# One GpSimd cast per head pair becomes a transfer, and the written-out order of all instructions is searched anew

## The chip, the cores and the metric

The kernel runs on one core of one Trainium2 chip. The metric is device microseconds of one execution. Three runs of the kernel before took 751.69, 751.89 and 752.91 us, with a median of 751.89 us.

The core's engines are TensorE (PE, with PEld for its weight loads), VectorE (DVE), ScalarE (ACT) and GpSimd (POOL). Each works through its own list of instructions in the order in which it stands; they meet only at semaphores. SyncE (SP) issues all transfers here. A row of SP is the issue of a transfer, and the transfer itself runs on the DMA engines.

## The reference

Two layers for 8 batches, 8 heads, 576 tokens, 64 columns per head. The first is causal attention with a bias from running sums of `s`; the second is a channel mix with 512 and 1024 columns:

```
scores = q @ k.T / 8                       # per head, 576 x 576
cum    = cumsum(max(s, 0))
scores = where(causal, -1e9, scores + min(cum_k - cum_q, 0))
x      = softmax(scores) @ v               # heads side by side: (8, 576, 512)
xk = mu_k * x + (1 - mu_k) * x_previous_token     # xr the same with mu_r
k  = relu(xk @ w_k)
out = sigmoid(xr @ w_r) * (k * k @ w_v)
```

Products are made exact by splitting: an operand is a rounded high part and a low part (what the rounding left), and two or three products of parts are added in PSUM.

## The kernel before, in words

**Attention.** The heads go in pairs. The first batch is done in two visits per pair (tiles A: queries 0 to 319; Z: the rest) and the second batch in one; these are the "plain" visits, whose weights TensorE turns (L1695) before it sums the values (`sum_plain`, L1816). From the third batch on (`b >= BY_DMA`, BY_DMA is 2) `split_scores` makes the scores (L1390), VectorE takes the row minimum (L1402), ScalarE the exponentials (L1417), ScalarE and VectorE write high and low halves of the weights (L1442, L1448), a transposing transfer turns them (L1535), and `sum_values` sums the values of both heads of the pair in one block of 32 matmuls (L1576).

**Keys and queries.** `split_qk` prepares a head: GpSimd (or ScalarE in the first two batches) rounds the keys into half of the tile `KH` (L1224, L1227, L1231), GpSimd writes the rest into the other half (L1235), and a second copy of the rounded keys goes into `KL` (L1241), beside three rows of running sums that a transfer brings (L1216). The queries are treated likewise (`G` at L1251 or L1255, `QL` at L1259). One product takes `KH` and `G`, the second `KL` and `QL`. The pair's heads are j = 0 and j = 1; `KH` and `KL` have three buffers each.

**Channel mix.** Tokens go in 18 chunks of 256. For the first two batches x goes through memory and is mixed and split by ScalarE and VectorE (L1993 to L2037); for the later ones `mix_pair` does it from the value sums (L1621 to L1669). `hidden` makes xk @ w_k (L2065, 96 matmuls of 256 columns per chunk), then relu (L2079), square and split; `gate` makes xr @ w_r (L2142); `output` makes the product with w_v (L2196), multiplies by the gate (L2207) and stores. The weights are first taken from 64-bit words, scaled by a power of two and split into halves (L940 to L1030).

**The order.** No engine's order is written by hand. The body of the kernel only records tasks in `Plan`: engine, planned length in ns, what it reads and writes, a due time. `pe`, `act`, `dve`, `pool` and `dma` turn columns into a planned length. `Plan.run` then makes the order: due times with a random shift drawn from SEED, PASSES rounds of `forward` (a list scheduler: at each step the engine that is free first takes the ready task with the earliest due time) and `backward` (new due times from the end), and then a nudge of the due times in one stretch for each number of CHAIN. The last `forward` gives each engine's order, and, for tasks with a choice (`or_act`, `or_dve`, `or_pool`), the engine. Where the planner sees TensorE idle ahead of the first two-part score product (L1315), it places a small matmul on the identity (`one_idle`, L540), whose result nobody reads.

The SP queue is in order too: each transfer's issue waits there for its sources and for the landing of a transfer eight before it.

Of the kernel before, what the change touches and what calls it, by code (L numbers as in the profile page):

```python
# [30 lines left out]
def f32(ap):  # L31
    return ap.bitcast(F32)
# [22 lines left out]
class Plan:  # L55
# [239 lines left out]
    def backward(self, start, on):  # L295
# [43 lines left out]
        return [-x for x in at]  # L339


    PASSES, SEED = 45, 67
    SHIFTS = 500.0, 2000.0, 5000.0, 10000.0
    NUDGES, SPANS = (300.0, 1000.0, 3000.0, 8000.0), (5000.0, 15000.0, 40000.0)
    LENGTH = 740000.0
    CHAIN = (
# [26 lines left out]
    )  # L373
    engines = ('DVE', 'ACT', 'POOL', 'SP', 'PE')
    LATER = 300.0
# [33 lines left out]
def forgetting_attention_then_channel_mix(  # L409
# [16 lines left out]
    nc = tc.nc  # L426

    B, H, D, S = q.shape
# [20 lines left out]
    def sbuf(shape, tag, bufs=1, dtype=F32):  # L449
        return plan.buffer(sb, shape, dtype, tag, bufs)  # L450
# [17 lines left out]
    def at_quarters(i, quarters):  # L468
        if quarters != (0, 0):
            plan.quarters[i] = quarters  # L470
        return i
# [12 lines left out]
    def pool(emit, reads, writes, n, extra, rate=0.8333, quarters=(0, 0)):  # L484
        return at_quarters(plan.add("POOL", n * rate + extra, emit, reads, writes), quarters)
# [12 lines left out]
    def dma(emit, reads, writes, ns):  # L498
        return plan.add("SP", 1.286 * ns, emit, reads, writes, land=1300)
# [75 lines left out]
    BY_DMA = 2  # L575
# [529 lines left out]
    ALL, A, Z = tuple(range(NQ)), (0, 1, 2), (3, 4)  # L1105
# [95 lines left out]
    def split_qk(b, hp, qs, k):  # L1201
# [4 lines left out]
        nq, nk = qs[0].n, k.n  # L1206
        found = []
        for j in range(2):
            own, other = slice(64 * j, 64 * j + 64), slice(64 - 64 * j, P - 64 * j)
            QQ, K = (sbuf([P, n], x, 3, F32R) for n, x in ((nq, "G"), (nk, "KH")))  # L1210
            QL, KB = (sbuf([P, S], x, 3, F32R) for x in ("QL", "KL"))
# [17 lines left out]
            else:  # L1229
# [7 lines left out]
                ),  # L1237
                [(k, j), (K, j)], [(K, 1 - j)], nk, 210, 1.99, (2 * j, 2 - 2 * j),
            )
            pool(  # L1240
                lambda own=own, KB=KB: nc.gpsimd.tensor_copy(KB.get()[0:64, 0:nk], k.get()[own]),  # L1241
                [(k, j)], [(KB, 0)], nk, 150, 0.8333, (2 * j, 0),
            )
            x = qs[j]
            if b < BY_DMA:
                or_pool(
# [300 lines left out]
    def sum_values(Ts, V):  # L1547
# [25 lines left out]
        def all_of_it():  # L1573
# [21 lines left out]
        columns = sum(n - start(y, kb) for y, x, kb in todo) + 4 * 64  # L1595
        pe(
            all_of_it, [(V, 0), (V, 1)] + list(dict.fromkeys(keys)), [found], columns, 64,
            1.05 / 2.4 + 256 / columns,
        )
        return found  # L1600

# [185 lines left out]
    def sum_plain(phs, rinv, V, xT, tiles):  # L1787
# [25 lines left out]
        def all_of_it():  # L1813
# [33 lines left out]
        columns = (q1 - q0) / 2 + sum(q1 - max(q0, kb * P) for kb in range(blocks))  # L1847
        pe(
            all_of_it, [V, ident16, (r16, 0), (r16, 1)] + keys, some, columns, 64,
            4 / 2.4 - 10 / columns,  # L1850
        )
        for a, e, sums, invs, off in places:
            def x(a=a, e=e):
# [653 lines left out]
```

## Time and profile before

| | |
|---|---|
| Median of three runs | 751.89 us |
| The profiled execution | 751.42 us, its span 749.7 us |
| Busy share of the span | PE 97%, DVE 79%, ACT 78%, POOL 66% |
| Granted TensorE clock, mean | 0.993 of full speed |
| Transfers | 109.93 MB, 63.5% of the 16 DMA engines' span in the main queue |

The share of busy time of an engine is an average over stages. TensorE's busy time is modelled at its ends (a matmul's row shows its latency, 0.27 to 0.51 us, while the next one starts earlier), so the distance from one start to the next tells what a matmul costs. Idle time of TensorE is shown in brackets in the order of time, with the engine and line that ended it. The clock column is the share of full speed that was granted: 1.00 is 2.4 GHz, 0.50 is 1.2 GHz.

### The profile page before, as it was taken

How to read it: one execution, taken by the hardware profiler on the slowest of the kernel's cores; microseconds unless marked ns; L12 is line 12 of the kernel's file. 1: busy time of each engine (PE TensorE's matmuls, PEld its weight loads, DVE VectorE, ACT ScalarE, POOL GpSimd, SP SyncE). 2: the span in 40 equal slices, each digit the busy share in tenths (PEclk: the TensorE clock that was granted, in tenths of full speed). 3: DMA queues.
4: the chain of work that ended last, by engine and by line, in shares of the span. 5: the costliest groups of instructions: out<-in, count | busy, mean ns of one | idle time of the engine just before them, and what ended most of it. 6: DMA issues, size and time to landing. Idle time of an engine off the chain costs nothing. (4 is left out here: it accounts for less than half of the span.)

```text
span 749.7 us, 17000 instructions
## 1 busy us (share of the span) xinstructions
PE 728.3 (97%) x5369; PEld 489.1 (65%) x5369; DVE 595.7 (79%) x1830; ACT 581.0 (78%) x1766; POOL 492.2 (66%) x609
## 2 busy tenths in 40 slices
PE   8989999999999989999999999999999999999998
PEld 7857866865566565757575757575757575755665
DVE  8999999888878988888898999988999796412322
ACT  6999998888979898988888878888888987312311
POOL 6798988588347778775986797769966971100000
PEclk9989999999999999999999999999999999999999
DMA  8866763359249987887788879778889685100000
GB/s 244 284 197 179 232 198 115 109 132 215 60 87 173 195 163 170 180 185 159 168 195 166 171 173 185 162 176 175 183 163 167 109 158 78 42 29 15 15 29 29
DMA packets 207339, 109.93 MB, mean 147 GB/s; under 512 B 178001, under 2 KB 183889, under 8 KB 207249
## 3 DMA queue, kind: packets, MB, share of 16 engines
q1 hardware_dynamic: 207248, 108.85, 63.5%
q8 instruction: 42, 0.69, 0.4%
q14 instruction: 49, 0.39, 0.2%
HBM read 54.09 MB, written 12.24 MB: 88 GB/s over the span
## 5 line engine op out<-in xcount | busy, mean ns | idle before, releaser
L2065 PEld LDWEIGHTS <-w_k 128*128 128x128 f16 x1728 | 160.1, 98 | 42.5 <-issue 13.9
L2065 PE MATMUL m<-xkh,w_k 128*128 128x256 f16 x976 | 182.9, 275 | 5.0 <-ACT xkh L2033 1.4
L2196 PE MATMUL m<-w_v,kh 128*128 128x512 f16 x528 | 166.7, 381 | 0.0
L2065 PE MATMUL m<-xkl,w_k 128*128 128x256 f16 x488 | 133.7, 276 | 2.3 <-POOL xkl L1666 1.3
L2196 PE MATMUL m<-w_v,kl 128*128 128x512 f16 x264 | 100.3, 382 | 0.0
L1235 POOL TENSOR_TENSOR KH<-raw,KH 64x576 fp32r<-64x576 f32 x64 | 91.0, 1422 | 4.6
L2196 PEld LDWEIGHTS <-kh 128*128 128x128 f16 x592 | 55.9, 98 | 56.7 <-issue 7.0
L1259 POOL TENSOR_TENSOR QL<-raw,G 64x576 fp32r<-64x576 f32 (+1 forms) x64 | 86.4, 1349 | 6.3 <-ACT G L1248 3.2
L2142 PE MATMUL m<-w_r,xrh 128*128 128x512 f16 x264 | 86.6, 381 | 1.5 <-ACT r L2079 1.2
L2170 POOL TENSOR_SCALAR g<-g,scale 128x512 f32<-128x512 f32 x24 | 18.8, 787 | 99.2 <-ACT g L2156 93.6
L1448 DVE SCALAR_TENSOR_TENSOR W<-s,rinv,W 128x64 f16<-128x64 f32 (+1 forms) x144 | 65.2, 457 | 12.7 <-ACT W L1442 11.3
L1442 ACT ACTIVATE W<-s,rinv 128x64 f16<-128x64 f32 (+1 forms) x144 | 64.5, 453 | 10.1 <-DVE rinv L1433 7.1
L1417 ACT ACTIVATE s<-s,nm 128x64 f32<-128x64 f32 (+2 forms) x144 | 61.6, 428 | 13.8 <-DVE nm L1402 9.3
L1390 PE MATMUL s<-KH,G 128*128 128x64 f32 (+3 forms) x192 | 68.7, 361 | 2.0 <-DVE W L1448 1.9
L1255 POOL CAST G<-raw 128x576 fp32r<-128x576 f32 x48 | 31.9, 665 | 52.1 <-PE s L1390 27.6
L1448 DVE SCALAR_TENSOR_TENSOR W<-t,rinv,W 128x320 f16<-128x320 f32 (+1 forms) x96 | 61.2, 645 | 5.7 <-ACT W L1442 4.6
L1390 PE MATMUL s<-KL,QL 67*128 67x64 f32 (+2 forms) x192 | 61.4, 330 | 0.0
L1417 ACT ACTIVATE t<-t,nm 128x320 f32<-128x320 f32 (+1 forms) x96 | 55.3, 576 | 7.0 <-DVE nm L1479 3.3
L1402 DVE CUSTOM_DVE_ANT_0 t<-t,lower 128x320 f32<-128x320 f32 (+1 forms) x96 | 57.2, 598 | 3.5 <-PE t L1390 2.6
L1442 ACT ACTIVATE W<-t,rinv 128x320 f16<-128x320 f32 (+1 forms) x96 | 56.6, 606 | 1.5 <-DVE rinv L1433 1.5
L1576 PE MATMUL pair<-T,V 128*64 128x512 f16 (+6 forms) x768 | 55.4, 295 | 0.7 <-ACT s L1417 0.4
L1576 PEld LDWEIGHTS <-V 128*64 128x64 f16 x768 | 37.3, 110 | 22.2 <-issue 5.0
(259 smaller groups left out, 1949.1 us busy)
## 6 DMA issues: line engine op xcount, KB each, us to landing
raw<-in_q SPq DMA_DIRECT2D x112, 144.0 KB
raw<-in_k SPq DMA_DIRECT2D x32, 288.0 KB
vn<-in_v SPq DMA_DIRECT2D x24, 384.0 KB
out<-g SPq DMA_DIRECT2D x35, 256.0 KB
wd<-in_moe_w_v SPq DMA_DIRECT2D x8, 512.0 KB
T<-W SPq DMA_TRANSPOSE x192
V<-in_v SPq DMA_DIRECT2D x8, 320.0 KB
wd<-in_moe_w_k SPq DMA_DIRECT2D x4, 512.0 KB
```

The lines of the kernel that those rows point to most:

```text
L1235: lambda own=own, other=other, K=K: nc.gpsimd.tensor_tensor(out=K.get()[other], in0=k.get()[own], in1=f32(K.get()[own]), op=ALU.subtract),
L1255: lambda x=x, QQ=QQ: nc.gpsimd.tensor_copy(QQ.get(), x.get()),
L1259: lambda x=x, QQ=QQ, QL=QL: nc.gpsimd.tensor_tensor(out=QL.get()[0:64, 0:nq], in0=x.get()[0:64], in1=f32(QQ.get()[0:64]), op=ALU.subtract,),
L1390: lambda x=x, G=G, K=K, r=r: nc.tensor.matmul(ps.get()[:m, :n], G.get()[:r, q : q + m], K.get()[:r, k0 : k0 + n], start=x == 0, stop=x == 1,),
L1402: lambda: nc.vector.tensor_tensor_reduce(out=ps.get()[:, :n], in0=ps.get()[:, :n], in1=mask(), scale=-SCALE, scalar=3.0e38, op0=ALU.add, o ...
L1417: lambda: nc.scalar.activation(ps.get()[:, :n], ps.get()[:, :n], AF.Exp, bias=nm.get()[:, i + o : i + o + 1], scale=-1.0, accum_out=sums.g ...
L1442: lambda: nc.scalar.activation(part(0), ps.get()[:, :n], AF.Copy, scale=rinv.get()[:, i : i + 1]),
L1448: lambda: nc.vector.scalar_tensor_tensor(out=part(1), in0=ps.get()[:, :n], scalar=rinv.get()[:, i : i + 1], in1=part(0), op0=ALU.mult, op1 ...
L1576: nc.tensor.matmul(ps.get()[64 * j : 64 * j + 64, a:e], V.get()[:, block[0], block[1], j], moving(j), start=first, stop=last, tile_positio ...
L2065: lambda u=u, f=f, c=c, n=n, w=w, x=x: nc.tensor.matmul(ps.get()[:, u * CT : (u + 1) * CT], weight["k", c, f // 4].get()[:, w, f % 4 * P : ...
L2142: lambda c=c, n=n, x=x, w=w: nc.tensor.matmul(ps.get(), row(1, x, c, place + tt * P, place + tt * P + P), weight["r", c, 0].get()[:, w], s ...
L2196: lambda f=f, i=i, x=x, w=w, ps=ps, columns=columns: nc.tensor.matmul(ps.get()[:, 0:n], x.get()[:, f, ts], weight["v", f, 0].get()[:, w, c ...
```

## The change

The second copy of the rounded keys of the first head (j = 0) of a pair, from the third batch on, is no longer cast by GpSimd from the loaded keys; a transfer issued by SP copies it from `KH`, where the rounded keys already stand. There are 6 batches with 4 pairs each, so 24 casts become 24 transfers of 64 rows of 2304 bytes (144 KB). The planned lengths of the two value sums change: for `sum_values` the constant falls from 256 to 163 ns; for `sum_plain` a rate with a small constant becomes a fixed 1597, 2176 or 3695 ns for the tiles A, Z or all. SEED, PASSES and CHAIN are new, so the planner starts elsewhere and takes other nudges.

```
-    PASSES, SEED = 45, 67
+    PASSES, SEED = 39, 210
     CHAIN = (
-        7000001, 7000002, 7000008, 7000030, 7000037, 7000049, 7000059, 7000088, 7000115,
...
+        5000000, 5000016, 5000017, 5000024, 5000041, 5000059, 5000061, 5000116, 5000146,
...
-            pool(
-                lambda own=own, KB=KB: nc.gpsimd.tensor_copy(KB.get()[0:64, 0:nk], k.get()[own]),
-                [(k, j)], [(KB, 0)], nk, 150, 0.8333, (2 * j, 0),
-            )
+            if b >= BY_DMA and j == 0:
+                dma(
+                    lambda own=own, K=K, KB=KB: nc.sync.dma_start(
+                        f32(KB.get()[0:64, 0:nk]), f32(K.get()[own])
+                    ),
+                    [(K, j)], [(KB, 0)], 410 * nk / S,
+                )
+            else:
+                pool(
+                    lambda own=own, KB=KB: nc.gpsimd.tensor_copy(KB.get()[0:64, 0:nk], k.get()[own]),
+                    [(k, j)], [(KB, 0)], nk, 150, 0.8333, (2 * j, 0),
+                )
...
         pe(
             all_of_it, [(V, 0), (V, 1)] + list(dict.fromkeys(keys)), [found], columns, 64,
-            1.05 / 2.4 + 256 / columns,
+            1.05 / 2.4 + 163 / columns,
         )
...
         pe(
             all_of_it, [V, ident16, (r16, 0), (r16, 1)] + keys, some, columns, 64,
-            4 / 2.4 - 10 / columns,
+            {A: 1597, Z: 2176, ALL: 3695}[tiles] / columns,
         )
```

Every engine's order changes; as a count, the same TensorE products are made, GpSimd has 32 instructions fewer (the 24 casts, and 8 that the planner gave to ScalarE and VectorE or took back), SP has 24 issues more, and the matmuls on the identity (L540 before, L537 after) go from 69 to 117. Three places follow. A line number after the change is 3 lower than before up to the edit in `split_qk`, and 5 higher behind it.

**First place: VectorE at the start.** `vn` is the input `s`, `xT` its running sums; `g` are the sums that the first score products need; `m` and `most_k` belong to the weights w_k; the ISA rows are the row minima of the first head's scores. Before:

```order
L653 TENSOR_SCALAR vn_115<-vn_115 64x576
L713 TENSOR_TENSOR g_166<-g_121,g_166 128x24
L660 SCALAR_TENSOR_TENSOR xT_176<-raw_113,vn_115 64x576
L671 TENSOR_TENSOR xT_176<-xT_176,w_v_00_210 64x576
L960 TENSOR_SCALAR m_225,most_k<-m_225 128x512
L1330 ISA W_249,nm_250<-s_168,lower 128x192
```

And now:

```order
L650 TENSOR_SCALAR vn_115<-vn_115 64x576
L657 SCALAR_TENSOR_TENSOR xT_172<-raw_113,vn_115 64x576
L957 TENSOR_SCALAR m_197,most_k<-m_197 128x512
L1121 TENSOR_REDUCE am_228<-V_138 128x1
L710 TENSOR_TENSOR g_223<-g_127,g_223 128x24
L668 TENSOR_TENSOR xT_172<-xT_172,w_v_00_211 64x576
L964 SCALAR_TENSOR_TENSOR m_197<-m_197,w_k_00_200 128x512
L668 TENSOR_TENSOR kh_281<-xT_172,w_v_00_258 64x576
L957 TENSOR_SCALAR m_283,most_k<-m_283 128x512
L1044 TENSOR_TENSOR most_k<-most_k 128x1
L964 SCALAR_TENSOR_TENSOR m_283<-m_283,w_k_10_288 128x512
L767 TENSOR_SCALAR most_k<-most_k 128x1
```

The sums `g` are behind the scan and a first weight's clamp, and the work on two weight blocks stands ahead of the first row minimum, which follows right behind these rows. On TensorE the matmuls on the identity fill this time: 21 stood ahead of the first product before, 54 now; 53 ahead of the first product with keys, 91 now.

**Second place: VectorE just ahead of the mix of the first chunk** (L2009 before, L2014 now). `xrh` and `w_r` belong to the weights w_r, `xp` is the mix, `unit` a row's scale. Before:

```order
L967 SCALAR_TENSOR_TENSOR xrh_771<-m_225,w_r_00_748 128x512
L1061 TENSOR_SCALAR unit<-unit 128x1
L1059 RECIPROCAL unit<-most_r 128x1
L1006 SCALAR_TENSOR_TENSOR w_r_00_860<-xrh_771,unit,w_r_00_860 128x512
L1061 TENSOR_SCALAR unit<-unit 128x1
L1378 RECIPROCAL inverses_314<-inverses_314 128x2
L1059 RECIPROCAL unit<-most_r 128x1
L967 SCALAR_TENSOR_TENSOR xrh_771<-m_288,w_r_00_762 128x512
L1006 SCALAR_TENSOR_TENSOR w_r_00_897<-xrh_771,unit,w_r_00_897 128x512
L2009 SCALAR_TENSOR_TENSOR xp_378<-w_v_00_261,mu_g_93,xp_378 128x256
```

And now:

```order
L964 SCALAR_TENSOR_TENSOR xrh_753<-m_197,w_r_00_699 128x512
L1335 ISA W_373,nm_374<-s_230,lower 128x288
L1335 ISA nm_374 128x1
L1058 TENSOR_SCALAR unit<-unit 128x1
L1056 RECIPROCAL unit<-most_r 128x1
L1335 ISA W_373,nm_374<-s_235,lower,nm_374 128x288
L1335 ISA nm_374 128x1
L1056 RECIPROCAL unit<-most_r 128x1
L771 TENSOR_SCALAR ranges<-ranges 128x1
L964 SCALAR_TENSOR_TENSOR xrh_753<-m_283,w_r_00_726 128x512
L2014 SCALAR_TENSOR_TENSOR xp_348<-w_v_00_263,mu_g_93,xp_348 128x256
```

Two low halves of w_r (L1006) are now behind the mix. Counted from the program's start, 171 VectorE instructions stood ahead of the mix, now 169. Ahead of TensorE's first hidden product stand 9 turns (L1695) fewer and 48 matmuls on the identity more; all else there is the same.

**Third place: TensorE at the first hidden products of the third chunk** (L2065 before, L2070 now; `xkh`, `xkl` are the chunk's halves). L2196, now L2201, are output products of the second chunk; L1390, now L1395, score products. Before:

```order
L1390 MATMUL s_173<-KH_563,G_565 128x192
L2065 LDWEIGHTS w_k_00_364
L2065 MATMUL m_225<-xkh_925,w_k_00_364 128x256
L1390 MATMUL s_173<-KL_538,QL_141 128x192
L2065 LDWEIGHTS w_k_00_364
L2065 MATMUL m_225<-xkl_934,w_k_00_364 128x256
L2065 LDWEIGHTS w_k_00_364
L2065 MATMUL m_225<-xkh_925,w_k_00_364 128x256
L2065 LDWEIGHTS w_k_00_507
L2065 MATMUL m_225<-xkh_925,w_k_00_507 128x256
```

And now:

```order
L1395 MATMUL s_235<-KH_624,G_597 128x192
L2070 LDWEIGHTS w_k_00_337
L2070 MATMUL m_197<-xkh_956,w_k_00_337 128x256
L1395 MATMUL s_235<-KL_570,QL_131 128x192
L2201 LDWEIGHTS kl_1244
L2201 MATMUL m_283<-w_v_00_1748,kl_1244 128x512
L2201 LDWEIGHTS kh_1103
L2201 MATMUL m_283<-w_v_00_1748,kh_1103 128x512
L2201 LDWEIGHTS kh_1103
L2201 MATMUL m_283<-w_v_00_1757,kh_1103 128x512
L2201 LDWEIGHTS kl_1244
L2201 MATMUL m_283<-w_v_00_1757,kl_1244 128x512
```

Before, the second chunk's output products were all ahead of the third chunk's hidden ones; now 11 of them stand among these.

## Rows read from the trace of the kernel before

**Rows 1.** Stretches of the span: us, busy us (x instructions) per engine, clock, DMA, GB/s
```profile
core 0: us, PE busy (x) PEld busy (x) DVE busy (x) ACT busy (x) POOL busy (x), PEclk, DMA share, GB/s
175.00:200.00 25.00, 21.71 (x152) 14.90 (x149) 21.55 (x68) 21.31 (x64) 13.35 (x20) 1.00 0.70 156
200.00:225.00 25.00, 23.41 (x167) 14.67 (x164) 19.81 (x61) 20.61 (x65) 12.08 (x14) 1.00 0.34 73
250.00:275.00 25.00, 21.36 (x167) 15.28 (x165) 23.72 (x81) 22.06 (x78) 16.21 (x20) 1.00 0.87 188
275.00:625.00 350.00, 347.97 (x2587) 228.89 (x2585) 309.55 (x954) 301.77 (x940) 276.64 (x311) 1.00 0.81 167
...
725.00:750.00 25.00, 21.62 (x152) 14.54 (x149) 6.49 (x11) 5.00 (x9) 1.52 (x2) 0.98 0.06 22
```

**Rows 2.** Groups by line, GpSimd: count, busy us, mean ns, idle us before
```profile
L1241 POOL CAST KL<-raw 64x576 fp32r<-64x576 f32 x64 | 45.1, 704 | 1.3
```

**Rows 3.** Order of time, GpSimd and TensorE, one head's KL: start, us, instruction
```profile
409.96 0.66 POOL L1241 CAST KL<-raw 64x576 fp32r<-64x576 f32 x1
...
420.96 0.37 PE L1390 MATMUL s<-KL,QL 67*128 67x448 f32 x1
```

**Rows 4.** One line's instructions: SP's issues of query loads, ns min/median/max
```profile
L1182 SPq DMA_DIRECT2D raw<-in_q x128: 465/541/2388, 15.6 to 584.8; - x128
```

**Rows 5.** Order of time, TensorE, the start
```profile
5.87 2.33 PE L540 MATMUL po<-ident 128*128 128x192 bf16 x26
...
39.13 0.47 PE L1315 MATMUL s<-KH,G 128*128 128x448 f32 x1
...
54.23 0.38 PE L2065 MATMUL m<-xkh,w_k 128*128 128x256 f16 x2
```

**Rows 6.** Stretches around the first hidden product, columns as in rows 1
```profile
39.00:54.00 15.00, 11.97 (x70) 7.87 (x67) 14.37 (x60) 14.12 (x43) 14.15 (x20) 0.77 0.61 199
54.00:66.00 12.00, 10.39 (x77) 7.28 (x76) 10.87 (x35) 10.71 (x29) 9.47 (x13) 0.86 0.55 164
```

**Rows 7.** Order of time, VectorE, ahead of the first mix
```profile
49.52 1.12 DVE L1006 SCALAR_TENSOR_TENSOR w_r<-xrh,unit,w_r 128x512 f16<-128x512 f32 x1
50.56 0.14 DVE L1061 TENSOR_SCALAR unit<-unit 128x1 f32<-128x1 f32 x1
...
51.34 0.74 DVE L1006 SCALAR_TENSOR_TENSOR w_r<-xrh,unit,w_r 128x512 f16<-128x512 f32 x1
52.00 1.00 DVE L2009 SCALAR_TENSOR_TENSOR xp<-w_v,mu_g,xp 128x256 f32<-128x256 f32 x2
...
53.99 0.76 DVE L2037 TENSOR_TENSOR xkl<-xp,xkh 128x256 f16<-128x256 f32 x2 [0.60 <-ACT xkh L2033]
```

**Rows 8.** Order of time, TensorE, third and fifth chunk: idle us and its end
```profile
182.03 0.27 PE L2065 MATMUL m<-xkh,w_k 128*128 128x256 f16 x1 [0.57 <-ACT xkh L2033]
...
183.35 0.27 PE L2065 MATMUL m<-xkl,w_k 128*128 128x256 f16 x1 [0.72 <-DVE xkl L2037]
...
262.06 0.27 PE L2065 MATMUL m<-xkh,w_k 128*128 128x256 f16 x1 [0.73 <-POOL xkh L1663]
262.95 0.27 PE L2065 MATMUL m<-xkl,w_k 128*128 128x256 f16 x1 [0.62 <-POOL xkl L1666]
```

**Rows 9.** Chain that ended last, a run of output products: start, us, count
```profile
407.74 3.25 PE m L2196 x15
```

**Rows 10.** Order of time, TensorE: one value sum of tiles A, one of a later batch
```profile
17.99 0.61 PE L1816 MATMUL t<-ident,r 64*64 64x64 bf16 x12
18.43 1.15 PE L1816 MATMUL po<-T,V 128*64 128x320 f32 x12
...
458.83 2.27 PE L1576 MATMUL pair<-T,V 128*64 128x512 f16 x32
```

**Rows 11.** Order of time, VectorE: the same small subtraction twice
```profile
17.82 0.16 DVE L1807 TENSOR_TENSOR r<-inverses,r 128x6 f16<-128x6 f32 x1
...
36.53 0.68 DVE L1807 TENSOR_TENSOR r<-inverses,r 128x6 f16<-128x6 f32 x1
```

47 rows, old and new, of the table CHAIN are left out of this document.

## The prediction

> **What bounds the kernel now.** I read the stretches of the span first, then the order of time on TensorE where the stretches show it idle, then who ended those idle times.
>
> The reader is to see three regimes. From 275 to 625 us TensorE is busy 347.97 of 350 us at full clock, while GpSimd, on which the cast stood, is busy 277 and VectorE 310 [rows 1]. There the time is the sum of TensorE's own work, and nothing that another engine saves can shorten it by more than 2.0 us. The end, from 625 us on, is TensorE's alone too: what is missing to 25 us in the last stretch, 3.4 us, is mostly the final multiplication and store [rows 1]. So time is lost in two places only.
>
> The first is the start. From 39 to 54 us TensorE is busy 11.97 of 15 us, at 0.77 of its clock, while VectorE, ScalarE and GpSimd are each busy over 14 of 15 [rows 6]. Idle 3.0, and 15 x (1 - 0.77) = 3.5 lost to the lower clock level (1.2 GHz, after TensorE had begun to wait): 6.5 us. From 54 to 66 us it is 1.6 idle plus 12 x 0.14 = 1.7: 3.3 us [rows 6]. TensorE waits there for VectorE, which prepares weights and attention at once.
>
> The second is 175 to 275 us, where the plain batches end and the split ones begin: three of its four quarters miss 3.3, 1.6 and 3.6 us of TensorE, 8.5 us in all, at full clock [rows 1], with VectorE and ScalarE busy some 80 to 95%. The waits are mostly for the halves of a chunk's x, as [rows 8] show.
>
> **The change part by part.**
>
> *The cast that goes.* 24 casts of 64x576. The group's mean is 704 ns, a late one alone takes 0.66 us [rows 2, 3]: 24 x 0.66 = 15.8 us of GpSimd. In rows 3 the copy is ready at 410.6 and the product that reads it starts at 421.0, 10.3 us later, so the cast was not on the path. It can be worth something only where TensorE waits for GpSimd; the two waits of rows 8 are 1.35 us, in the stretch where the casts of the third batch stand. I take -0.3, between 0 and -2.0.
>
> *The transfer that comes.* 24 issues on SP. A query load of the same 144 KB takes SP 541 ns in the middle [rows 4], so 13 us more of SP's queue over some 450 us. No row shows a copy from one on-chip tile to another with such rows, so its run is bounded: below 0 if the 10.3 us of lead hide all of it, which also must hold the new wait (the issue waits for GpSimd's rounding into `KH`, which stands ahead of the rest of the head's work); above, if what is queued on SP behind the waiting issue, the transposing transfers that the value sums need, comes late by the 0.54 us of one issue each time, 24 x 0.54 = 13 us, less what TensorE has to do meanwhile. I take 0, nearest to rows 3. If that cover were gone (a lead under 3 us), each pair would show a wait on the `KL` product.
>
> A rule of the Trainium skill bears on the cast. The row: one subtraction of 6 columns takes 0.16 us once and 0.68 us another time, with nothing else different than what runs beside it [rows 11]. The rule ("SBUF — State Buffer", section "SBUF: two separate sides"): VectorE and GpSimd share one pair of ports as an exclusive lock, so a VectorE instruction with two on-chip inputs stands still while a reading GpSimd instruction runs. The trace agrees with it as far as the two rows go. By the rule 15.8 us of casts gone give VectorE back part of this, and the sum would fall by up to the 2.0 us that TensorE idles from 275 to 625; by the rows of that stretch it falls by nothing, and I take the latter.
>
> *The planned lengths.* No engine's work changes by them. The planner had a value sum of tiles A at 1.2 us where the rows give 18.43 + 1.15 - 17.99 = 1.59, and one of a later batch at 2.39 where they give 2.27 [rows 10]. The plan is now nearer to the chip. Price by itself: 0. What it buys is in the order.
>
> *The new order, start.* First, 48 matmuls on the identity more (117 for 69), all ahead of the first plain score product (L1315). 26 of them took 2.33 us [rows 5], 0.09 each: +4.3 us. They stand where the first place of the order shows weights ahead of the first head, so TensorE would reach L1315 not at 39.1 but at 43.4 us. What is late next is not TensorE but VectorE: the first hidden product started at 54.2 right behind the mix [rows 5, 7]. In the second place of the order two low halves of w_r no longer stand ahead of the mix. They cost 1.12 + 0.74 = 1.9 us [rows 7], less about 0.2 of overlap with their followers and some 0.3 for small rows that came ahead: 1.4. VectorE has hardly a gap up to there (14.37 of 15 us), so the first hidden product should start at 54.2 - 1.4 = 52.8. From 43.4 that is 9.4 us. TensorE's work in it was 15.1 - 6.5 = 8.6 before, and is 1.0 less by the nine turns that are now behind (0.11 each): 7.6. So 1.8 us are lost there instead of 6.5: -4.7. The start up to the first hidden product comes to +4.3 - 4.7 = -0.4. If VectorE's chain does not come earlier, it is +1.0; if TensorE simply keeps its distance from L1315 to the first hidden product, +4.3.
>
> *54 to 66 us.* A TensorE that is less starved ahead of it should keep its clock better. I take back half of the 1.7 us of clock: -0.8, between -3.3 (all of it) and +2.
>
> *175 to 275 us.* In the third place of the order 11 output products now stand among the first hidden ones of the third chunk. One costs 3.25 / 15 = 0.217 us [rows 9], so 2.4 us of work where TensorE waited 0.57 and 0.72 us for that chunk's halves [rows 8]. I take -0.9 of these 1.3. The rest of the 8.5 us may go or come back elsewhere with the new order; the bounds are -5 and +4, about half of it either way.
>
> *Sum.* -0.4 - 0.8 - 0.9 - 0.3 = -2.4 us. The profiled execution took 751.4 us (span 749.7 and 1.7 around it), so 749.0; it lay 0.5 under the median of the three runs, 751.9, so **749.5 us** as a median.
>
> **The rivals.**
>
> *No change.* TensorE has the same products to make, and a search can shift waits as easily as remove them: the start's -0.4 and new waits in the second region for the old ones, sum between -1.5 and +1.5, 751.9 us. For it: TensorE's place in attention against chunk work is nearly the same in both orders. Against it: two visible waits get cover.
>
> *Slower: the identity matmuls are not given back.* Place: the start. If VectorE, by taking weights first, then makes the attention rows late, TensorE's distance from L1315 to the first hidden product stays near what its work and waits were, and the first hidden product starts at about 58 us instead of 53. Price up to +4.3: 756.2 us. It decides once that product starts later than about 56 us. For it: VectorE, ScalarE and GpSimd are all full there [rows 6], so any row put ahead delays another. Against it: the rows ahead of the mix are fewer than before, and their sum is what set its start.
>
> *Slower: copies hold up SP.* The upper bound above, about half of it seen: +6.5, 758.4 us. For it: SP's queue is in order and the copy waits. Against it: 10.3 us of lead, and TensorE with other work queued.
>
> *Much faster.* All 3.3 us after 54 and most of the second region go as well: -0.4 - 2 - 5 = -7.4, 744.5 us. For it: the planner's lengths are truer. Against it: nothing but the third place shows it.
>
> **How the numbers follow.** Forecast (-1.5 to -4.5) 0.36; much faster 0.14; no change 0.29; identity matmuls 0.16; copies 0.05. A difference under 0.2%, 1.5 us, cannot be told from no change here. So faster 0.50, same 0.29, slower 0.21. The range from 744.5 to 755.5 leaves out the copies, the worst of the identity rival, and part of the much faster case; the likeliest case's own range is 747.4 to 750.4.
>
> **What would show it.** In the changed kernel's order of time: L1320 (L1315 before) first at about 43.4 us and the first hidden product at about 52.8, with TensorE idle and clock loss in between near 2 us; in the 39 to 66 us stretch a higher clock share; 175 to 275 us with under 7.5 us of TensorE idle; 275 to 625 us as full as before with GpSimd's busy time some 12 us lower; no wait of L1395 for a transfer. A first hidden product after 56 us, waits of value sums for transposing transfers, or new waits of over 2 us past 275 us would make the prediction wrong.

## The result, and the profile after

The changed kernel takes 757.26 us (median of 9 runs, 755.92 to 762.67); the kernel before took 752.00 beside it. The ratio is 1.0072 (95% interval 1.0050 to 1.0093): slower by 5.3 us, where 749.5 was forecast and 755.5 was the upper end. The profiled execution shown below is the median run: 757.26 us, span 755.3, against 751.4 and 749.7 before.

The same stretches of the span as in [rows 1, 6], of the changed kernel:
```profile
core 0: us, PE busy (x) PEld busy (x) DVE busy (x) ACT busy (x) POOL busy (x), PEclk, DMA share, GB/s
39.00:54.00 15.00, 13.58 (x118) 9.59 (x117) 14.16 (x67) 14.39 (x50) 13.18 (x21) 1.00 0.76 223
54.00:66.00 12.00, 9.71 (x86) 7.36 (x86) 11.82 (x28) 10.25 (x28) 8.76 (x12) 1.00 0.67 204
175.00:200.00 25.00, 23.68 (x160) 15.53 (x160) 23.27 (x74) 23.01 (x75) 9.97 (x18) 1.00 0.68 138
200.00:225.00 25.00, 23.92 (x162) 13.65 (x162) 19.89 (x60) 22.10 (x66) 16.42 (x18) 1.00 0.55 108
250.00:275.00 25.00, 22.60 (x178) 16.25 (x177) 23.21 (x72) 21.90 (x74) 16.57 (x21) 1.00 0.83 174
275.00:625.00 350.00, 342.38 (x2521) 224.09 (x2519) 309.82 (x944) 299.56 (x930) 257.67 (x282) 1.00 0.84 172
```
The places that the prediction worked on did improve: TensorE is at full clock from 39 us on, and the three quarters of 175 to 275 us that are shown miss 4.8 us of TensorE where they missed 8.5. The stretch that it took for safe lost: 275 to 625 us misses 7.6 us of TensorE where 2.0 were missing [rows 1], while GpSimd is 19.0 us less busy.

For a sharper view, each TensorE matmul is given the median time from its start to the next start, by line and width, as the trace of before has it where nothing idles in between; the multiplications of the identity count nothing. All kernels then have 739.1 us of TensorE work, and the time at which W us of it are done, less W, is what is lost up to there. Us of work are not us of the span: in the kernel before, 60 us of work are done at 78 us of the span, 100 at 116, 175 at 189, 250 at 269, 275 at 294, 425 at 441 and 500 at 512. The table has the loss (e1 is the first kernel under "The experiments", and so on by the label's number) against the profiled execution of before (two profiled executions of the same order differ by up to 0.8 here, from the start on; the columns e1 to e15 are experiments of the next section):
```
 W us   after    e1    e2    e3    e9   e10   e11   e13   e15
   10   +4.1   +3.9  +0.3  +5.1  +4.5  +4.1  +3.9  +3.8  +4.4
   60   -0.8   -1.3  +0.4  +0.3  -0.7  -0.9  -1.2  -1.6  -1.7
  100   +2.8   +2.4  +0.4  +4.0  +3.1  +2.7  +2.4  +2.0  +1.5
  175   +2.9   +2.5  +0.2  +4.1  +3.2  +2.8  +2.5  +2.1  +1.6
  250   -1.5   -1.8  +0.3  -0.3  -1.2  -1.5  -1.8  -2.3  -2.4
  275   +1.2   +1.5  +0.3  +2.4  +1.5  +0.4  +1.5  -0.4  -0.5
  400   +0.5   +1.4  +0.9  +2.7  +0.9  -0.0  +1.3  -1.2  -1.2
  425   +3.0   +7.5  +1.5  +7.3  +1.5  +0.0  +2.5  -1.0  -1.0
  475   +3.5   +7.5  +1.5  +7.3  +2.0  +0.8  +3.1  -0.5  -0.5
  500   +5.4   +7.8  +1.5  +8.9  +3.7  +1.1  +3.4  -0.2  -1.0
  700   +5.6   +7.5  +1.6  +8.9  +3.7  +0.9  +3.2  +0.6  +0.1
```
Read down the first column, in us of work: 4.1 us late at once, all of it back by 60, 3.6 lost by 100, 4.4 won from 175 to 250, then 2.7, 2.5 and 1.9 lost in three short places. Three rows of TensorE, in order of time (start, us, instruction, idle us ahead and what ended it), show the longest wait of each:
```profile
277.15 0.38 PE L2147 MATMUL m<-w_r,xrh 128*128 128x512 f16 x1 [1.34 <-ACT r L2084]
...
437.75 0.48 PE L1395 MATMUL s<-KH,G 128*128 128x448 f32 x1 [1.52 <-DVE W L1453]
...
511.92 0.62 PE L1581 MATMUL pair<-T,V 128*64 128x512 f16 x4 [1.69 <-DMA T<-W]
```
The last is a value sum that waits for a transposing transfer. SP's queue in the changed kernel (issue, us, kind, tiles) has the key copy, then a load, then two transposes, without gaps:
```profile
505.78 0.53 SPq L1239 DMA_DIRECT2D KL<-KH  x1
506.36 0.46 SPq L1213 DMA_DIRECT2D KL<-cum_d  x1
506.87 2.56 SPq L1540 DMA_TRANSPOSE T<-W  x2
```
The other two lead back to VectorE. This is VectorE's order of time in the changed kernel ahead of the wait at 437.75:
```profile
430.99 0.42 DVE L1671 TENSOR_TENSOR xrl<-pair,xrh 128x256 f16<-128x256 f32 x1
...
432.17 3.64 DVE L1671 TENSOR_TENSOR xkl<-wd,xkh 128x256 f16<-128x256 f32 x1
...
437.42 0.28 DVE L1453 SCALAR_TENSOR_TENSOR W<-s,rinv,W 128x64 f16<-128x64 f32 x1
```
And GpSimd's order of time beside it:
```profile
426.49 1.77 POOL L1150 TENSOR_SCALAR vn<-vn,scale 128x768 f32<-128x768 f32 x2
428.21 1.58 POOL L1156 CAST V<-vn 128x768 f16<-128x768 f32 x2
429.77 3.24 POOL L1158 TENSOR_TENSOR V<-vn,V 128x768 f16<-128x768 f32 x2
433.00 0.89 POOL L1150 TENSOR_SCALAR vn<-vn,scale 128x768 f32<-128x768 f32 x1
433.87 0.78 POOL L1671 TENSOR_TENSOR xkl<-wd,xkh 128x320 f16<-128x320 f32 x1
434.64 0.89 POOL L1150 TENSOR_SCALAR vn<-vn,scale 128x768 f32<-128x768 f32 x1
435.58 0.91 POOL L1156 CAST V<-vn 128x768 f16<-128x768 f32 x1
```
A subtraction of 256 columns takes 0.42 us with one input in the accumulators (`pair`) and 3.64 here with both in the on-chip memory; the only other one of this kind in this kernel, at 370.14 us, took 0.61. It ends, at 435.81, just after one of GpSimd's back-to-back instructions (435.53). All that stands behind it on VectorE, the half of the probabilities that TensorE wants included, comes later by about these 3 us. The Trainium skill's rule ("SBUF — State Buffer", section "SBUF: two separate sides": an instruction of VectorE with two on-chip inputs and a reading one of GpSimd shut each other out for a whole instruction) agrees with these rows, and they show more than one instruction's length. Ahead of the wait at 277.15 VectorE, in the changed kernel, has two rows of the same kind:
```profile
268.79 2.41 DVE L2112 SCALAR_TENSOR_TENSOR kl<-kh,r 128x512 f16<-128x512 f16 x1
...
273.94 2.47 DVE L2112 SCALAR_TENSOR_TENSOR kl<-kh,r 128x512 f16<-128x512 f16 x1
```
They free `r`, which ScalarE's L2084 overwrites and TensorE then waits for. In the kernel before such rows took less there:
```profile
268.96 1.44 DVE L2107 SCALAR_TENSOR_TENSOR kl<-kh,r 128x512 f16<-128x512 f16 x1
...
273.56 0.87 DVE L2107 SCALAR_TENSOR_TENSOR kl<-kh,r 128x512 f16<-128x512 f16 x1
```
They too ran beside GpSimd instructions that followed each other closely; what decides how many of these go first is not shown.

### The profile page after: what moved, and what is told of

The parts are those of the page before. It is cut to its first block, busy times and chain, and to the rows that moved or that the text cites. A ratio compares the mean times of both kernels' runs of the same rounds, so it can differ in the third digit from the quotient of the medians.

```text
span 755.3 us, 17147 instructions
## 1 busy us (share of the span) xinstructions
PE 731.6 (97%) x5417; PEld 489.5 (65%) x5417; DVE 602.6 (80%) x1832; ACT 584.6 (77%) x1773; POOL 472.7 (63%) x577
## 4 chain that ended last, share of the span: by engine, by line
PE 67%; DVE 14%; ACT 9%; issue 5%; DMA 2%; POOL 2%; SPq 0%; DVEq 0%; ACTq 0%; POOLq 0%
PE m L2201 19%; PE m L2070 14%; PE m L2147 7%; PE pair L1581 6%; PE t L1395 4%; PE s L1395 4%; PE t L2070 2%; PE s L2070 2%; PE t L2201 2%; PE t L1700 2%; ACT W L1447 2%; DVE W L1335 1%; PE s L1298 1%; PE s L1309 1%; DVE W L1453 1%
## 5 line engine op out<-in xcount | busy, mean ns | idle before, releaser
L2070 PEld LDWEIGHTS <-w_k 128*128 128x128 f16 x1728 | 159.6, 98 | 38.5 <-issue 12.6
L2070 PE MATMUL m<-xkh,w_k 128*128 128x256 f16 x976 | 180.9, 274 | 3.6 <-ACT xkh L2038 1.3
L2201 PE MATMUL m<-w_v,kh 128*128 128x512 f16 x528 | 167.5, 381 | 0.8 <-ACT g L2161 0.7
L2070 PE MATMUL m<-xkl,w_k 128*128 128x256 f16 x488 | 133.0, 274 | 1.7 <-POOL xkl L1671 1.6
L2201 PE MATMUL m<-w_v,kl 128*128 128x512 f16 x264 | 100.2, 381 | 0.2 <-DVE kl L2112 0.2
L1232 POOL TENSOR_TENSOR KH<-raw,KH 64x576 fp32r<-64x576 f32 x64 | 93.1, 1454 | 8.2 <-ACT KH L1221 3.3
L2201 PEld LDWEIGHTS <-kh 128*128 128x128 f16 x592 | 55.9, 98 | 56.8 <-issue 6.5
L1453 DVE SCALAR_TENSOR_TENSOR W<-s,rinv,W 128x64 f16<-128x64 f32 (+2 forms) x144 | 65.4, 457 | 8.7 <-ACT W L1447 7.1
L1395 PE MATMUL s<-KH,G 128*128 128x64 f32 (+3 forms) x192 | 69.0, 359 | 3.2 <-DVE W L1453 3.0
L1447 ACT ACTIVATE W<-s,rinv 128x64 f16<-128x64 f32 (+2 forms) x144 | 64.7, 455 | 8.5 <-DVE rinv L1438 7.1
L1395 PE MATMUL s<-KL,QL 67*128 67x64 f32 (+2 forms) x192 | 61.9, 331 | 0.0
L1228 POOL CAST KH<-raw 64x576 fp32r<-64x576 f32 x48 | 32.2, 671 | 35.4 <-PE s L1395 27.0
```

Of the source, the lines that this page charges most:

```text
L1232: lambda own=own, other=other, K=K: nc.gpsimd.tensor_tensor(out=K.get()[other], in0=k.get()[own], in1=f32(K.get()[own]), op=ALU.subtract),
L1395: lambda x=x, G=G, K=K, r=r: nc.tensor.matmul(ps.get()[:m, :n], G.get()[:r, q : q + m], K.get()[:r, k0 : k0 + n], start=x == 0, stop=x == 1,),
L1447: lambda: nc.scalar.activation(part(0), ps.get()[:, :n], AF.Copy, scale=rinv.get()[:, i : i + 1]),
L1453: lambda: nc.vector.scalar_tensor_tensor(out=part(1), in0=ps.get()[:, :n], scalar=rinv.get()[:, i : i + 1], in1=part(0), op0=ALU.mult, op1 ...
L2070: lambda u=u, f=f, c=c, n=n, w=w, x=x: nc.tensor.matmul(ps.get()[:, u * CT : (u + 1) * CT], weight["k", c, f // 4].get()[:, w, f % 4 * P : ...
L2201: lambda f=f, i=i, x=x, w=w, ps=ps, columns=columns: nc.tensor.matmul(ps.get()[:, 0:n], x.get()[:, f, ts], weight["v", f, 0].get()[:, w, c ...
```

## The experiments

Each median is against the kernel before on the same chip (752.2 to 752.5), with the 95% interval of the ratio; the rows and the table are of one profiled execution each. Line numbers in the rows are those of the experiment's own kernel and run a few past the changed one's.

**Copies and order taken apart.** Both orders were kept row for row; only what the 24 rows emit was exchanged.
```diff
 (e1: the changed order with casts; e2, in the order of before, the reverse)
-    lambda own=own, K=K, KB=KB: nc.sync.dma_start(
-        f32(KB.get()[0:64, 0:nk]), f32(K.get()[own])
-    ),
+    lambda own=own, KB=KB: nc.gpsimd.tensor_copy(KB.get()[0:64, 0:nk], k.get()[own]),
```


> The changed kernel's order, kept row for row; only the 24 transfers from KH to KL are put back as GpSimd casts, each at the transfer's place. Theory 'copies hold up SP' (they delay transposing transfers and take queue time; 24 x 0.53 us of issue on SP): 752 to 755 us, the 1.7 us wait of a value sum for a transfer near 512 us gone. Rival 'order': the transfers cost nothing, the new order of the chunk work does: 757 us, within 1, and the waits of 0.5 to 1.5 us between 275 and 625 us stay where they are.

> The order of the kernel before, kept row for row; only its 24 casts of the first head's second copy from batch 3 on are made transfers from KH at the same place of the program (where the cast stood ahead of the rounding, right behind the rounding). Theory 'copies hold up SP': 754 to 757 us, with new waits of value sums for transposing transfers. Rival 'order': 752 us, within 1, TensorE still under 2.5 us idle from 275 to 625 us.

```
                   casts              transfers
order of before    752.35             753.74 (1.0011 to 1.0029)
changed order      758.94 (1.0073 to 1.0101)   757.26 (1.0050 to 1.0093)
```
The order is the cause: with casts alone it costs 6.6 us. The copies cost 1.4 us in the order of before, a tenth of the bound of 13; part of it is a value sum that waits for its transposes, as the rival had it (order of time on TensorE, e2; the same sum at 430.68 us in the kernel before did not wait):
```profile
432.70 0.81 PE L1587 MATMUL pair<-T,V 128*64 128x512 f16 x6 [0.67 <-DMA T<-W]
```
In the changed order the median is 1.7 lower with them, but the two intervals overlap. The profiled executions differ the same way (last row of the table: +7.5 and +5.6), and show how. Neither theory had that: with the cast back in GpSimd's queue the caught subtraction took 5.03 us, and TensorE's granted clock came to 0.86 of full over the 25 us around that wait, and to 0.50, the lower level of 1.2 GHz, in the 5 us from 440 us on, behind it. VectorE's caught row in e1:
```profile
433.05 5.03 DVE L1669 TENSOR_TENSOR xkl<-wd,xkh 128x256 f16<-128x256 f32 x1
```
TensorE's wait behind it, in e1:
```profile
440.03 0.74 PE L1393 MATMUL s<-KH,G 128*128 128x448 f32 x1 [3.49 <-DVE W L1451]
```
And the stretch of e1 around it, with the columns of the first table (0.86 is the clock):
```profile
425.00:450.00 25.00, 21.51 (x144) 13.01 (x143) 21.72 (x48) 17.62 (x52) 20.75 (x24) 0.86 0.61 127
```

**The identity multiplications and the start.**
```diff
 def one_idle():
     idles.append(None)
+    if not 33 < len(idles) <= 102:
+        return
     nc.tensor.matmul(
...
-        start=len(idles) == 1,
+        start=len(idles) == 34,
```


> The changed kernel's order without 48 of its 117 multiplications of the identity (33 of the first 54, the last 15), so 69 as before; nothing reads their sums. Theory 'VectorE sets the first hidden product': it still starts at 52.4 us, TensorE only waits longer ahead of it; total within 1 us of the changed kernel's 757.3. Rival 'not given back': 4.4 us less, 752.9.

761.38 us (1.0110 to 1.0137): slower than with them, and both expectations missed. TensorE is no earlier at 10 us of work but 1.0 later. The first score product waits (order of time on TensorE, e3):
```profile
7.86 0.39 PE L1300 MATMUL s<-kl,g 128*128 128x192 f32 x2 [2.62 <-ACT g L710]
```
In the changed kernel the same product starts at 7.68, behind the multiplications. So the multiplications fill a wait for the forget gate, which the new order loads behind a block of weights and subtracts on VectorE at 7.72 us instead of 5.21. Without them the clock is 0.79 from 6 to 14 us, where it is 1.00 in the changed kernel. The first hidden product was 1.1 us later too, and the 1.2 us of delay met the caught subtraction of 432 us at a worse moment (4.42 us): +4.6 between 400 and 425 us of work.

> The changed kernel with 69 multiplications of the identity as in the third experiment, and the forget gate's transfer ahead of the first block of weights, its two ScalarE steps and its VectorE subtraction ahead of the scan, as in the kernel before. Theory 'the gate, not the multiplications, starts the first score products late, and VectorE takes it back': the first score product at about 5.2 us instead of 7.9, TensorE some 3 to 4 us ahead of the third experiment's up to 35 us, then idle; the first hidden product at 52 to 53 us, the total within 1.5 us of the third experiment's 761.4. Rival 'the late start stays': 3 to 4 us under it, 757.5.

```diff
 (e6: on top of e3; x goes ahead of y. 1, 5, 6, 7: the gate's transfer and its three steps)
+for x, y in ((1, 33), (5, 11), (6, 11), (7, 11)):
+    order.remove(x)
+    order.insert(order.index(y), x)
```
759.06 us (1.0079 to 1.0110). The first score product comes at 5.15 us, but the next kind waits at 11.35 us for a query, which also stands behind weights on SP (TensorE, e6):
```profile
11.35 0.82 PE L1314 MATMUL s<-KH,xkh 128*128 128x192 f32 x4 [1.62 <-DMA xkh<-in_q]
```
At 10 us of work TensorE is 1.1 us ahead of the third experiment, not 3 to 4. Of the late start nothing lasts in any kernel with this order: the loss is under 0.5 us at 60 us of work.

**The search's numbers.**
```diff
-PASSES, SEED = 39, 210
+PASSES, SEED = 45, 67   (and the chain of the kernel before)
```


> The changed kernel with the search's numbers (passes, seed, chain) of the kernel before; the transfers and the corrected lengths stay, so the planner makes a third order. Theory 'copies hold up SP': 755 to 757 us. Rival 'order': the numbers were found for another set of lengths, so the order is one that no search has chosen: anything from 751 to 760; a distance of over 3 us from the changed kernel, either way, would show that orders of the same work differ by as much as the change did.

780.74 us (1.0360 to 1.0388), far outside both. Seeds that were chosen for one set of lengths give, with 60 tasks changed (36 value sums have new lengths, 24 casts are transfers), an order 28 us slower on the chip. It is lost all along: by the measure of the table 5 us by 60 us of work, 14 by 250, 19 by 400 and 27 at the end.

**Single rows moved.** Rows are moved in the order as in the sixth experiment.

> The changed kernel with three instructions a little later on their own queues: VectorE's 128x256 xkl subtraction that took 3.64 us at 432 us goes behind the halves of the probabilities (L1453) that TensorE waited 1.52 us for at 437.75; the key copy and the cum row issued at 505.8 and 506.4 us on SP go behind the two transposing transfers. Theory 'local waits of the order' (a VectorE instruction with two on-chip inputs caught between back-to-back GpSimd instructions; one copy ahead of a transpose): the waits at 437.75 and 511.9 us go, 757.3 - 1.5 to 2.5 - up to 1.0 = 753.5 to 756.0. Rival 'TensorE's neighbours are full anyway' (the waits move to the next instruction): 757, within 1.

758.98 us (1.0071 to 1.0096). All three rows moved were others than those named: VectorE's subtraction of 576 columns at 442.75 us, and a key copy with its cum row at 527 us. The row of 3.64 us and SP's queue at 505.8 us stood as before, and so did the waits behind them (1.53 and 1.47 us). The run says nothing on either.

> The changed kernel with one VectorE instruction moved: the 128x256 xkl subtraction (3.64 us at 432.17, 0.42 elsewhere) goes behind the two L1453 rows at 437.4 and 437.9, its result being needed much later (the fifth experiment moved another row of that line by mistake). Theory 'it is caught between back-to-back GpSimd instructions and holds up VectorE's queue': the wait of TensorE of 1.52 us at 437.75 goes, 757.3 - 1.5 to 2.5 = 754.8 to 755.8, VectorE's rows behind it some 3 us earlier. Rival 'VectorE is late there anyway': the wait stays over 1 us, 757.

```diff
+for x, y in ((4967, 5487),):      # xkl of 432 us, ahead of the mixed-in row of 439 us
```
755.26 us (1.0019 to 1.0045), 2.0 less, as the theory had it. VectorE's rows are 2.2 us earlier, and TensorE does not wait at L1398. VectorE's order of time in e9:
```profile
435.24 0.28 DVE L1456 SCALAR_TENSOR_TENSOR W<-s,rinv,W 128x64 f16<-128x64 f32 x1
...
436.37 1.20 DVE L1674 TENSOR_TENSOR xkl<-wd,xkh 128x256 f16<-128x256 f32 x1
```
TensorE's in e9:
```profile
435.71 0.55 PE L1398 MATMUL s<-KH,G 128*128 128x448 f32 x1
```


> The changed order with all 24 casts in place of the transfers (the first experiment, 758.9) and the subtraction of the ninth moved. Theory: the first experiment lost 4.5 us between 427 and 440 us to that subtraction (5.03 us there) and the clock that fell behind the wait, and has no wait for a transfer at 512, so 754 to 755.5, level with the ninth or under it: the transfers are worth nothing. Rival 'the casts cost GpSimd time wherever it is full': 757 or more.

755.09 us (1.0021 to 1.0044): 3.9 under the first experiment, level with the ninth. Once that row is out of the way, casts and transfers cost the same.

> As the ninth, and two more repairs of the changed kernel: the second head pair's value halves on GpSimd at 271.8 and 274.2 us (and the load that waits for them) go behind two later rows, and the 3 key copies issued at 470, 488 and 506 us are GpSimd casts again. Theory 'local waits of the order, and the copies at one place': the wait of 1.34 us at 277.15 shrinks by about 1, the one of 1.69 us at 511.9 goes: 752 to 754. Rival 'each repair is paid by the next wait': 755 to 757.

```diff
+for x, y in ((4967, 5487), (3544, 3475), (3545, 3475), (3620, 3475)):
 (and casts again where len(plan.tasks) in (5877, 6404, 6535))
```
753.84 us (1.0010 to 1.0028). The copies that became casts are those at 488, 506 and 527 us. The wait of 1.69 us at 511.9 is gone, as it is with all casts in the first experiment; the one of 1.34 is down to 0.57 (TensorE, e10):
```profile
276.32 0.38 PE L2154 MATMUL m<-w_r,xrh 128*128 128x512 f16 x1 [0.57 <-ACT r L2091]
```
Of the 5.3 us, 3.4 are back by three repairs past 250 us.

> The tenth with two VectorE rows of the first attention (the reciprocal L1383 at 60.19 us, for which ScalarE idles 1.28 us, and the maximum L1335 at 61.30) ahead of three low halves of w_r (L1003), of which two stand 1.5 us still in all. Theory 'those halves, caught between GpSimd rows, start the loss from 60 us on': TensorE's wait of 1.21 us at 60.8 goes, and 1 to 1.5 us of it lasts: 752.5 to 753 where the tenth took 753.8. Rival 'VectorE is full from 66 to 100 us, so its work sets the time there and order within it does not': the wait goes and comes back later, 753.8 within 0.5.

```diff
+(566, 149), (905, 149)            # reciprocal and score maximum ahead of w_r's low halves
```
752.64 us (0.9994 to 1.0012): level with the kernel before. The gain is at 60 us of work already (-1.6, where the tenth has -0.9); from there to 100 it loses 3.6 like the tenth. ScalarE had idled there behind three such halves, two of them caught. The changed kernel's VectorE there:
```profile
56.58 3.69 DVE L1003 SCALAR_TENSOR_TENSOR w_r<-xrh,unit,w_r 128x512 f16<-128x512 f32 x3
60.19 0.15 DVE L1383 RECIPROCAL inverses<-inverses 128x2 f32<-128x2 f32 x1
```
And its ScalarE:
```profile
60.38 0.20 ACT L1808 CAST r<-inverses 128x4 f16<-128x4 f32 x1 [1.28 <-DVE inverses L1383]
```


> The thirteenth, and four VectorE rows that nothing needs before about 150 us (three maxima over values, L1121, at 73 to 95 us, 0.54 to 0.82 us each, and the small L1131 behind them) go to 125 to 142 us, where VectorE has room (8.3 of 10 us busy from 120 to 130). Theory 'VectorE is full from 66 to 100 us': up to 2.2 us less than the thirteenth, of which 1 to 2 is seen: 751 to 752, level with the kernel before or under it. Rival 'the loss there is not VectorE's': the thirteenth, within 0.5.

754.53 us (1.0020 to 1.0040), worse than the thirteenth, and neither expectation. The three maxima stood at 80.0, 93.9 and 101.3 us. From 76 to 117 us, where the 3.6 us are lost, VectorE is then busy 39.15 us for 40.58 in the thirteenth, and TensorE 39.41 for 39.45; the moved rows cost 2 us where they went. So the amount of VectorE work there is not the cause.

> The thirteenth with four more VectorE rows moved, each from just ahead of a row that TensorE waits for: an am maximum (0.81 us at 75.0) behind the maxima of the scores, a reduction of weights (0.69 at 85.4) behind two score maxima, a half of probabilities (0.68 at 205.3) ahead of a mixed-in row, and another (0.54 at 511.2) ahead of a mixed-in row that waits 0.70 us for GpSimd. Theory 'local waits of the order add up': 0.8 to 1.4 us less than the thirteenth's 752.6, 751.2 to 751.8, under the kernel before. Rival 'paid at the next wait', as in the twelfth: 752.6 within 0.4.

751.84 us (0.9988 to 1.0006): level with before. It is 0.8 under the thirteenth, which ran on another chip; the intervals overlap.

> The fifteenth with three more VectorE rows moved: a kl row (0.70 us) that TensorE waited 0.93 us for at 207.6 goes into the 0.71 us in which VectorE waited for ScalarE at 205.5, and two am maxima (0.82 and 0.81 at 516.0 and 517.3) behind the halves of probabilities that TensorE waited 0.74 us for at 518.4. Theory 'local waits of the order add up': 0.6 to 1.4 us less than the fifteenth's 751.8, 750.4 to 751.2, faster than the kernel before beyond the measurement. Rival 'paid at the next wait': 751.8 within 0.4.

753.06 us (1.0002 to 1.0020): no gain, and 0.9 over what the rival allowed. Nothing here beats the kernel before by more than can be measured.

**The order of before, repaired and spliced.**

> The kernel before with four rows moved between 263 and 271 us: VectorE's am reduction (0.82 us) and mixed-in row (0.82) behind the xrl subtractions that TensorE waited 0.96 us for at 265.60, ScalarE's second xrh cast ahead of an exponential, and VectorE's kl row (1.44 us, 0.69 elsewhere) behind the two xrl rows that TensorE waited 0.98 us for at 270.85. Theory 'rows put ahead of what TensorE waits for set its waits': 1.0 to 1.9 us less, 750.1 to 751.0. Rival 'paid at the next wait' (r and kl come later): 752, within 0.7.

752.91 us (0.9991 to 1.0009): both waits, 1.9 us together, are gone, and the time is the same, near the rival's. But no next wait pays for them: in the profiled execution TensorE's granted clock is 0.84 and 0.82 in the two halves of 260 to 270 us, where the kernel before had 1.00, and that is 1.7 us. Whether the moves brought that about is not shown.

> The kernel before, casts and all, with its order written out: its own up to about 186 us, the changed kernel's from there to about 269 us, its own again to the end. Theory 'order, place by place': the changed order gained 4 to 5 us between these two places and lost the rest elsewhere, so 752 - 4.4 = 747.5 (746.5 to 749). Rival 'what is gained there was paid ahead of it' (the changed order comes to 186 us with VectorE and ScalarE some 2 to 3 us further on, which cost it the time from 66 to 100 us): 750 to 752.

> As the seventh, and also the changed kernel's order up to about 77 us, then the kernel before's to 186 us. Theory 'order, place by place': another 1.0 us less than the seventh, 746.5. Rival 'paid ahead or later': the rows that the changed order leaves for later come now between 77 and 100 us, and the 1 us is lost there: equal to the seventh or up to 3 us more.

In both the order is written out as a list: one kernel's first rows, then the other's that are not yet issued. 765.95 us (1.0131 to 1.0184) and 766.51 (1.0174 to 1.0202); the profiled execution of the seventh is its fastest, 760.87. The seams cost more than the middle could win. At the first one:
```profile
207.80 0.74 PE L1557 MATMUL s<-KH,G 128*128 128x448 f32 x1 [4.05 <-DVE W L1615]
```
Behind the second one TensorE is busy 19.94 of 25 us from 275 to 300 us. At a seam the rows come that the one order had done by then and the other had not. That part of the gain from 175 to 250 us was paid for earlier, as the rival had it, fits this but is not shown by it: the waits are the splice's own.

## Why the prediction was wrong

- *The step that failed* is the reading of 275 to 625 us: "There the time is the sum of TensorE's own work, and nothing that another engine saves can shorten it by more than 2.0 us", with "So time is lost in two places only". True of shortening; I read it as if nothing could lengthen it either, and priced the new order at three places only. It made waits of 1.3 to 1.7 us at three new ones, +2.7, +2.5 and +1.9 on the table, and lost 3.6 between 60 and 100 us of work (about 77 to 118 us of the span), which the prediction did not price at all. The sign I had named for being wrong, new waits of over 2 us past 275 us and value sums waiting for transposes, is what came, except that no single wait reached 2 us.
- *The rule weighed* (VectorE and GpSimd shut each other out): I set its effect at nothing, by TensorE's busy share of the whole stretch. One caught row took 3.0 us more than its like, and moving it gave 2.0. VectorE's total was no guide: what mattered was which row was caught and what stood behind it.
- *Start.* The first plain score product came at 43.41 (43.4 forecast) and the first hidden one at 52.36 (52.8). The mix came at 50.61 for 52.00, so the 1.4 of VectorE's chain was right. The +4.3 was right in size by luck and wrong in cause: the multiplications fill waits for the gate and the queries, and without them the product at 43.41 comes at 44.48 and the time is longer. That it is given back held.
- *54 to 66 us*: -0.8 forecast; 3.3 us lost before, 2.3 after, so -1.0.
- *175 to 275 us*: -0.9 forecast for two waits at the third chunk, and both are gone. The stretch as a whole won more, 3.7 us of idle time in the quarters shown. The +2.7 on the table belongs to 269 to 294 us of the span; most of it stands behind the two caught `kl` rows (waits of 0.51 us at 271.95 and 1.34 at 277.15).
- *Casts and copies*: -0.3 and 0 forecast, +1.4 together in the order of before, within the bounds, and nothing that can be measured in the repaired order (ninth and eleventh). The "copies" rival was right in kind, at 0.7 to 1.7 us a place, not 6.5.
- *The rivals* lacked the one that came: a search's order makes single new waits in the stretch that is full. "TensorE's place in attention against chunk work is nearly the same" says nothing of VectorE's order just ahead of it, which the comparison of orders had on show.
- *Open*: the 3.6 us between 60 and 100 us of work. Only 1.3 of it shows as idle time (TensorE is busy 39.43 of 41 us from 77 to 118 us of the span, 40.73 before). The fifteenth lost 3.2 there, a difference within that of two executions; the amount of VectorE work is excluded, the rest is not explained.

## What to carry to other kernels

A stretch in which TensorE is full has little to win from a faster helper, and much to lose by a new order: compare, in the two orders, what stands on each helper just ahead of the rows that TensorE reads, and price one caught row there, not the mean. When an edit and a new search come together, take them apart by keeping the order and exchanging only what a row emits. Here the numbers of a search did not carry over to other planned costs; ten rows moved by hand from the trace, and three copies made casts again, won back what the new order lost, and no more.

## What the runs showed of the hardware that was not expected

- A VectorE instruction with both inputs on chip took 3.64 and 5.03 us (0.61 elsewhere) beside back-to-back GpSimd instructions of 0.8 to 1.6 us: several of them went first.
- A copy of 64x576 from one on-chip tile to another takes SP 534 ns to issue (median of 24), as a load from memory does [rows 4], and 24 of them in place of casts cost 1.4 us in all in an unchanged order.
- 48 multiplications of the identity at the start are worth about 1 us of TensorE's start: without them its clock is 0.79 from 6 to 14 us, with them 1.00.
